# An SSM-convolution and SwiGLU gate, forward and backward in one program: the DFT matrices of the backward convolution turned on TensorE, its first loads in another order, one store on another queue

## The chip, the cores and the metric

The program runs on one core of a Trainium2 chip. The metric is the device time of one execution in microseconds (us), the median of the timed runs, lower is better. A profile is one execution taken by the hardware profiler; its span runs from the first to the last instruction.

## The reference

Only the part that the change touches is shown. `x` is 2048 tokens by 576 channels; `K` is a convolution kernel of 2048 taps for each channel, made from the SSM parameters.

```python
def _fwd_reference(...):
    xn = _layernorm(x, axis=-1)
    s = _A_ref(xn, ...)                 # y = causal convolution of xn with K (by FFT), plus xn * Dskip
    g = _silu(_B_ref(xn, w1, w3, w2))   # out = (silu(xn w1) * (xn w3)) w2, F = 4608
    return x + s * g

def reference(...):
    _out, _vjp = jax.vjp(_f, A_u, A_A_re, ..., B_w1, B_w3, B_w2)
    return (_out, *_vjp(grad_out))      # the output and the gradients of all twelve inputs
```

The backward pass needs `gs = grad_out * g`, the gradient that enters the convolution. From it come the gradient of `xn` and that of `K`, both by the same kind of convolution.

## The kernel before, in words

The convolution is done in blocks of 512 tokens (`LS`), four blocks (`NB`), each block of four tiles (`KT`) of 128 tokens. A block's spectrum is a product with cosine and sine matrices of 512 by 512, held in SBUF as tiles of 128 partitions by 4 by 512 in bf16. There are two kinds. `dC` and `dS` belong to the kernel's own transform (line 868) in the forward pass; the backward pass needs the same two matrices transposed, for the way back from the spectrum to taps (`idft_pair`, line 893). `cCS` belongs to the transform of the tokens; it is folded, 512 KB in all, is kept in DRAM as `CS_dram` from the prologue on, and is loaded again for the backward pass as `cCSb` (line 1301).

The program runs through these stages, with the times of the profiled execution:

- a prologue, then the first SwiGLU product (`ffn_hidden`, lines 1120 and 1128: `pgu`) woven with the making of the taps and, from about 400 to 530 us, with the forward convolution (`ssm_conv`, `conv_half`). For each half of the channels, `inverse(m)` for m = 3, 2, 1, 0 adds up products of spectra on VectorE (`V`) and goes back to tokens on TensorE (line 903). ScalarE copies one PSUM tile out (`ev`, line 1023), VectorE adds and subtracts the other (lines 1025 and 1026).
- the second SwiGLU product (`ffn_output`, about 545 to 697 us): for each of 16 token tiles i, 72 matmuls at line 1216 with a transposed load of H (`hcA`, `hcB`, `hcC`) as weights. `finish` follows on VectorE and stores `gs_t` (line 1237) and the output `o0` (line 1244).
- the backward pass (`backward`, from about 685 us): 18 groups of the SwiGLU gradients (`phase6_group` and what follows it), into which the backward convolution is woven by quarters g = 0 to 3 of the channels (`conv_bwd_quarter`), and then the parameter gradients and the input's gradient (line 1965) to the end.

The convolution's quarter 0 begins with the transform of `gs` (`dft_folded`, lines 879 to 884): twelve groups of four matmuls for blocks 0, 1 and 2, each group copied out by ScalarE (line 884); block 3 comes later, since its tokens (`gs_end`, kept in SBUF) are the last made. `fold` (lines 1375 to 1380) makes the difference `gm` and the sum `gs` of mirrored tiles on VectorE first. `a` and `az` are the two parts of the stored input spectrum (`UH_dram`); `spectrum_variants` (lines 909 to 911) prepares them on VectorE.

Every engine works its instructions in program order. The order of the work on each engine comes from priorities: `self.at(us)` sets a due time for what is recorded next, and `issue_after` holds an instruction behind another. A DMA is issued by an engine's queue, and an engine's queue (SP's, which carries most loads and stores, and POOL's) holds everything behind an issue that waits. DMAs of SP's queue share eight completion semaphores in turn, so each issue also waits for the landing of the DMA eight before it.

The transposed matrices `idC` and `idS` come about like this before the change: `dft_kernel_matrices` stores `dC` and `dS` to `D_dram`, and `dft_turn_kernel` loads them back with eight transposing DMAs, one behind each H load of tiles 5 and later.

`et_ps` is a PSUM tag with three buffers of one bank each. The forward convolution and the backward convolution both take their PSUM tiles from such a pool of three, and `pgu` has two buffers of two banks.

Of the kernel before, what the change touches and what calls it, by code (L numbers as in the profile page):

```python
# [13 lines left out]
FP32 = mybir.dt.float32  # L14
BF16 = mybir.dt.bfloat16
I32 = mybir.dt.int32
I16 = mybir.dt.int16
P = 128
# [82 lines left out]
class K:  # L101
# [722 lines left out]
    def dft_kernel_matrices(self, sb, half):  # L824
        nc, LS = self.nc, self.cfg.LS
        if half == 0:
            self.dC = self.matp.tile([P, 4, LS], BF16, name="dC")
            self.dS = self.matp.tile([P, 4, LS], BF16, name="dS")
        t = sb.tile([P, 2], FP32, name="dft_tk")
        fr = sb.tile([P, 2, LS], FP32, name="dft_frk")  # L830
        q = sb.tile([P, 2, LS], FP32, name="dft_qk")
        sl = slice(2 * half, 2 * half + 2)
        for i in range(2):
            with self.tc.issue_after(self.v_last.ins):
                nc.vector.tensor_scalar(out=t[:, i:i + 1], in0=self.ptok[:], scalar1=float((2 * half + i) * P), scalar2=None,
                                        op0=ALU.add)
            nc.scalar.activation(out=fr[:, i, :], in_=self.irow[:, 0:LS], func=ACT.Identity, scale=t[:, i:i + 1])
        self.wrap_turns(nc.vector, fr, q, 2.0 * LS)
        self.turn_sines(nc.scalar, self.dS[:, sl], self.dC[:, sl], fr, q)
        for i in range(2):  # L840
            nc.vector.tensor_copy(out=self.dS[:, 2 * half + i, 0:1], in_=self.sgnt[:])
        if half == 1:
            self.D_dram = self.dram.tile([2, 4, P, LS], BF16, name="D_dram")
            for m, mat in enumerate((self.dC, self.dS)):
                nc.sync.dma_start(out=self.D_dram[m].rearrange("i p k -> p i k"), in_=mat[:])

    def dft_turn_kernel(self):
        mats = []
        for m, tag in enumerate(("dC", "dS")):
            t = self.matp.tile([P, 4, self.cfg.LS], BF16, name="i" + tag, tag=tag)  # L850
            for i in range(4):
                with self.tc.issue_after(self.hc_loads[5 + 4 * m + i].ins):
                    self.nc.sync.dma_start_transpose(out=t[:, :, i * P:(i + 1) * P], in_=self.D_dram[m, i])
            mats.append(t)
        self.dC, self.dS = mats

    def dpieces(self):
        D = self.cfg.D
# [72 lines left out]
    def ssm_conv(self, T0, TC, ps, ps1):  # L931
        with self.pool(name="c_u", bufs=1) as up, \
                self.pool(name="c_k", bufs=1) as kp, \
                self.pool(name="c_raw", bufs=2) as rp, \
                self.pool(name="c_y", bufs=2) as ypool, \
                self.pool(name="c_tmp", bufs=2) as tp, \
                self.pool(name="c_s", bufs=3) as spool, self.pool(name="c_e", bufs=2) as epool:
            self.s_stores = []
            half = [self.conv_half(h, T0, kp, up, rp, ypool, tp, spool, epool, ps) for h in range(2)]
            NB = self.cfg.NB  # L940
            for b in range(NB):
                half[0]["dft"](b)
                half[0]["take"](b)
            for m in (3, 2):
                half[0]["inverse"](m)
            for m in (1, 0):
                half[1]["dft"](1 - m)
                half[0]["inverse"](m)
            for b in range(NB):
                if b > 1:  # L950
                    half[1]["dft"](b)
                half[1]["take"](b)
            for m in range(NB - 1, -1, -1):
                half[1]["inverse"](m)

    def conv_half(self, h, T0, kp, up, rp, ypool, tp, spool, epool, ps):
        nc, cfg = self.nc, self.cfg
# [187 lines left out]
    def ffn_output(self, T0, TB):  # L1145
        nc, cfg = self.nc, self.cfg
# [8 lines left out]
        with ExitStack() as es:  # L1155
# [64 lines left out]
            def finish(st):  # L1220
# [9 lines left out]
                with self.tc.issue_after(self.h_last.ins):  # L1230
# [3 lines left out]
                nc.vector.tensor_tensor(out=got, in0=gos[:], in1=e[:], op=ALU.mult)  # L1234
                gs_t = ip.tile([P, D], BF16, name="gs_t")
                nc.vector.tensor_tensor(out=p4(gs_t[:]), in0=n4(go_t[:]), in1=n4(g[:]), op=ALU.mult)
                nc.sync.dma_start(out=self.GS_dram[:, :, i, :].rearrange("g p d -> p g d"),
                                  in_=gs_t[:].rearrange("p (g d) -> p g d", g=4))
                if i >= LT - cfg.KT:
                    nc.scalar.copy(out=self.gs_end[:, i - LT + cfg.KT], in_=gs_t[:, 0:D // 4])  # L1240
                nc.vector.tensor_tensor(out=n4(g[:]), in0=p4(s_t[:]), in1=n4(g[:]), op=ALU.mult)
# [39 lines left out]
    def ssm_bwd_conv(self, T0, TQ, ps):  # L1281
        nc, cfg = self.nc, self.cfg
        D, LT = cfg.D, cfg.LT
        self.gK_dram = self.dram.tile([4, 2, P // 2, D // 64, 2, 2, 8 * LT], BF16, name="gK_dram")
        with self.pool(name="b_g", bufs=1, side="right") as self.bgp, \
                self.pool(name="b_k", bufs=1, side="right") as kp, self.pool(name="b_z", bufs=2, side="right") as zp:
            self.at(T0)
            self.lcol = kp.tile([P, LT], FP32, name="lcol")
            nc.vector.tensor_scalar(out=self.lcol[:], in0=self.irow[:, 0:LT], scalar1=float(P),
                                    scalar2=self.ptok[:, 0:1], op0=ALU.mult, op1=ALU.add)  # L1290
            nc.vector.tensor_scalar(out=self.lcol[:], in0=self.lcol[:], scalar1=1.0 / 512, scalar2=None, op0=ALU.mult)
            self.at(T0 - 100)
            self.dft_turn_kernel()
            W = D // 4
            for b in range(cfg.NB):
                kp.tile([P, 1, 2, cfg.KT, W], BF16, name=f"a2_{b}")
                kp.tile([P, 1, cfg.KT, W], BF16, name=f"az_{b}")
            kp.tile([P, cfg.NB, 2, W], BF16, name="gm")
            self.cCS = kp.tile([P, 2, 2, cfg.LS], BF16, name="cCSb")
            with self.tc.issue_after(self.hc_loads[5].ins):  # L1300
                nc.sync.dma_start(out=self.cCS[:], in_=self.CS_dram[:].rearrange("m i p k -> p m i k"))
            for g in range(4):
                yield from self.conv_bwd_quarter(g, kp, zp, ps, T0 + g * TQ, TQ)

# [38 lines left out]
    def conv_bwd_quarter(self, g, kp, zp, ps, T0, TQ):  # L1343
# [9 lines left out]
        for b in range(NB - 1 if g == 0 else 1):  # L1353
            ts = slice(b * KT, (b + 1) * KT) if g == 0 else slice(0, LT)
            if g == 0:
                self.at(T0 - 170 + 40 * b)
            nc.sync.dma_start(out=gs[:, ts], in_=self.GS_dram[g, :, ts])
        self.at(T0 if g else T0 - 100)
        for b in range(NB):
            A2[b] = kp.tile([P, 1, 2, KT, W], BF16, name=f"a2_{b}")  # L1360
            Az[b] = kp.tile([P, 1, KT, W], BF16, name=f"az_{b}")
            sync = Chain(self.tc, nc.sync)
            sync.prev = (ld if b else None) if g else self.hc_loads[2 * b + 4]
            sync.dma_start(out=A2[b][:, 0, 0], in_=self.UH_dram[g, b, :, 0])
            ld = sync.dma_start(out=Az[b][:, 0], in_=self.UH_dram[g, b, :, 1])
        G = [None] * NB
# [814 lines left out]
```

## Time and profile before

| | us |
|---|---|
| median of the timed runs (3) | 1768.03 |
| lowest and highest of them | 1760.42 and 1770.57 |
| the profiled execution's own time | 1755.63 |
| its span | 1753.7 |
| VectorE busy, share of the span | 1360.8, 78% |
| ScalarE busy | 890.6, 51% |
| TensorE busy 680 to 720 us | 29.5 of 40 |
| TensorE busy 720 to 760 us | 38.4 of 40 |

The profiled execution is shorter than all three timed runs. Busy times of TensorE count a matmul from its issue to its modelled end, so neighbours overlap; the distance between the starts of equal instructions is the better measure of a pace. Times within the program, such as "at 707 us", count from the span's start.

### The profile page before, as it was taken

The numbers are of one execution on the slowest core, as the hardware profiler recorded it, in microseconds if no ns is written. First come the engines' busy times: TensorE is split into PE (matmuls) and PEld (weight loads), VectorE is DVE, ScalarE is ACT, GpSimd is POOL, SyncE is SP. The second block draws the span as 40 slices with busy tenths as digits, with TensorE's granted clock in tenths as the row PEclk, the third lists the DMA queues.
The fourth block names the chain that finished last, engine by engine and source line by source line (L and its number), as shares of the span: only waits on it lengthen the run. The fifth ranks groups of instructions, "written<-read, shape, count | busy, mean of one in ns | idle before, by whom it ended". The sixth has DMA issues, their size and how long they took to land. (4 is left out here: it accounts for less than half of the span.)

```text
span 1753.7 us, 34702 instructions
## 1 busy us (share of the span) xinstructions
PE 1623.7 (93%) x13708; PEld 1196.8 (68%) x13765; DVE 1360.8 (78%) x2221; ACT 890.6 (51%) x1437; POOL 329.5 (19%) x530
## 2 busy tenths in 40 slices
PE   5889998999998999799999999999999998899997
PEld 2444444454545777678888888888888776678886
DVE  7658888879694555786976989759999975888675
ACT  4878889876862113665765657565444511001001
POOL 3101111112232110111011011111111133132132
PEclk9989999999999999999999999999999999999999
DMA  7779999978799998757676585679999999999991
GB/s 208 271 249 361 357 347 358 367 254 253 254 275 239 238 227 180 217 172 215 193 197 190 156 241 177 177 207 277 242 252 230 214 256 201 236 247 220 211 232 47
DMA packets 633769, 414.02 MB, mean 236 GB/s; under 512 B 427478, under 2 KB 578246, under 8 KB 628998
## 3 DMA queue, kind: packets, MB, share of 16 engines
q1 hardware_dynamic: 586780, 285.38, 65.8%
q0 software_dynamic: 32704, 114.32, 19.8%
q10 hardware_dynamic: 14122, 12.10, 2.5%
q8 instruction: 108, 1.77, 0.4%
q14 instruction: 55, 0.45, 0.1%
HBM read 130.88 MB, written 191.94 MB: 184 GB/s over the span
## 5 line engine op out<-in xcount | busy, mean ns | idle before, releaser
L1120 PE MATMUL pgu<-wmB_w,xnT 128*128 128x512 bf16 x1101 | 269.5, 379 | 5.6 <-ACT gu_t L1133 2.4
L1965 PEld LDWEIGHTS <-acts 128*128 128x128 bf16 x2304 | 226.0, 99 | 64.2 <-DMA acts<-GG_dram 3.3
L1913 PEld LDWEIGHTS <-xn_bf 128*128 128x128 bf16 x2304 | 224.9, 98 | 34.9 <-issue 8.6
L1496 DVE TENSOR_TENSOR pr_q<-et_ps,pz 128x1024 f32<-128x1024 f32 x144 | 176.0, 1222 | 35.3 <-PE et_ps L1491 24.4
L1965 PE MATMUL px<-wT,acts 128*128 128x288 bf16 x1472 | 192.9, 289 | 0.0
L1120 PEld LDWEIGHTS <-xnT 128*128 128x128 bf16 x1152 | 106.9, 98 | 120.4 <-issue 21.3
L1499 DVE TENSOR_REDUCE S_all<-pr_q 128x32 f32<-128x1024 f32 x144 | 175.3, 1217 | 3.1
L1852 PE MATMUL ph<-w2T,goT 128*128 128x256 bf16 x1440 | 171.1, 273 | 5.2 <-ACT gh L1855 5.2
L1852 PEld LDWEIGHTS <-goT 128*128 128x128 bf16 x1440 | 139.3, 98 | 23.3 <-issue 7.3
L1894 PE MATMUL pgw<-go_o,h_n 128*128 128x288 bf16 x1152 | 148.8, 286 | 0.0
L1133 ACT CAST gu_t<-pgu 128x1024 bf16<-128x1024 f32 x144 | 147.3, 1023 | 0.0
L1913 PE MATMUL pgw<-gu_n,xn_bf 128*128 128x256 bf16 x1152 | 133.7, 275 | 6.9 <-ACT gw L1896 6.3
L1894 PEld LDWEIGHTS <-h_n 128*128 128x128 bf16 x1152 | 112.0, 98 | 29.4 <-issue 2.0
L1913 PE MATMUL pgw<-gg_n,xn_bf 128*128 128x256 bf16 x1152 | 130.5, 273 | 0.0
L1132 ACT ACTIVATE s_t<-pgu 128x512 bf16<-128x512 f32 x144 | 87.8, 610 | 83.7 <-PE pgu L1120 44.4
L1141 POOL DMA_DIRECT2D GUF_dram<-gu_t x72 | 65.5, 910 | 339.7 <-ACT gu_t L1133 312.4
L1965 PE MATMUL px<-wA,acts 128*128 128x288 bf16 x832 | 110.3, 289 | 5.2 <-DMA acts<-GG_dram 2.7
L1916 ACT CAST gw<-pgw 128x512 bf16<-128x512 f32 x72 | 42.6, 591 | 140.8 <-PE pgw L1913 139.8
L1855 ACT CAST gh<-ph 128x512 bf16<-128x512 f32 x144 | 83.0, 608 | 58.7 <-PE ph L1852 50.9
L2032 ACT ACTIVATE go<-gx 128x576 bf16<-128x576 f32 x15 | 10.2, 683 | 190.8 <-DVE gx L2013 190.8
L1136 DVE TENSOR_TENSOR h_t<-s_t,gu_t 128x1024 bf16<-128x1024 bf16 x72 | 49.5, 688 | 47.8 <-ACT gu_t L1133 46.8
L1897 POOL DMA_DIRECT2D out_dram<-gw x36 | 20.2, 562 | 345.5 <-ACT gw L1896 269.7
(329 smaller groups left out, 3019.4 us busy)
## 6 DMA issues: line engine op xcount, KB each, us to landing
GUF_dram<-gu_t POOLq DMA_DIRECT2D x72, 512.0 KB, 5.6
H_dram<-h_t SPq DMA_DIRECT2D x72, 256.0 KB, 5.5
Q_dram<-q_k SPq DMA_DIRECT2D x36, 512.0 KB, 3.9
gg_n<-GUF_dram POOLq DMA_DIRECT2D x18, 1024.0 KB, 6.0
h_n<-GUF_dram POOLq DMA_DIRECT2D x18, 1024.0 KB, 8.6
GG_dram<-gg_n SPq DMA_DIRECT2D x36, 512.0 KB, 10.3
GU_dram<-gu_n SPq DMA_DIRECT2D x36, 512.0 KB, 5.3
E_dram<-E_k SPq DMA_DIRECT2D x54, 256.0 KB, 2.3
```

The lines of the kernel that those rows point to most:

```text
L1120: ins = nc.tensor.matmul(pt, lhsT=xnT[:, c, ts], rhs=wm[w][:, c, :], start=(q == 0 and c == 0), stop=(q == 1 and c == nfull - 1))
L1132: nc.scalar.activation(out=s_t[:, :, q, :], in_=pg.rearrange("p (g f) -> p g f", g=ng), func=ACT.Silu)
L1133: nc.scalar.copy(out=gu_t[:, :, :, q, :], in_=pgu[:].rearrange("p k (g f) -> p k g f", g=ng))
L1136: self.h_last = nc.vector.tensor_tensor(out=h_t[:].rearrange("p t (g f) -> p g t f", g=ng), in0=s_t[:], in1=gu_t[:, 1], op=ALU.mult)
L1141: self.u_stores[step] = nc.gpsimd.dma_start(out=self.GUF_dram[fb * ng:(fb + 1) * ng, :, :, i0:i0 + NT, :].rearrange("g p k t f -> p k g (t ...
L1496: nc.vector.tensor_tensor(out=pr[:].rearrange("p r k e -> p r (k e)"), in0=T[x][:].rearrange("p k z d a -> p (k z d a)")[:, None].to_broad ...
L1499: nc.vector.tensor_reduce(out=self.S_all[:, :, d0:d0 + 4], in_=pr[:].rearrange("p r k (d a) -> p (r k) d a", d=4), op=ALU.add, axis=AX.X)
L1852: self.pe_last = nc.tensor.matmul(ph[j][:, k, :].rearrange("p (a f) -> p a f", f=P), lhsT=lw, rhs=rh, start=(n == 0), stop=(n == nfull))
L1855: self.sc(lambda: nc.scalar.copy(out=gh[:, j], in_=ph[j][:]))
L1894: self.pe_last = nc.tensor.matmul(pgw[pi_][:, 0:pw], lhsT=hn[:, tt, fl * P:(fl + 1) * P], rhs=go_o[:, tt, po:po + pw], start=(tt == 0), st ...
L1913: self.pe_last = nc.tensor.matmul(pw_[:, c % 2], lhsT=self.xn_bf[:, tt, c * P:(c + 1) * P], rhs=nat[:, tt, :], start=(tt == 0), stop=(tt = ...
L1965: self.pe_last = nc.tensor.matmul(px[pi_][:, 0:pw], lhsT=acts[i][:, ai, fi, :], rhs=w[:, po:po + pw], start=(n == 0), stop=(n == len(steps ...
```

## The change

Three edits that go together:

1. `D_dram`, its two stores and the eight transposing loads are gone. `dft_turn_kernel` now transposes each matrix in place: 16 transposes of 128 by 128 on TensorE (data as weights, identity as the moving operand) into two `et_ps` tiles, seen as bf16, and two copies of 128x1024 by ScalarE back into the matrix. It is called twice in the forward convolution's second half: after `inverse(3)` for `dC`, and after `inverse(2)` for `dS`, each with a due time 8 us behind that inverse's.
2. The backward convolution's first loads: `cCSb`, which was issued behind the eight loads of `a` and `az`, comes ahead of them, right behind the three loads of `gs`.
3. The store of `gs_t` for the last tile (i = 15) goes to GpSimd's queue; the other fifteen stay on SP's.

```diff
-        if half == 1:
-            self.D_dram = self.dram.tile([2, 4, P, LS], BF16, name="D_dram")
-            for m, mat in enumerate((self.dC, self.dS)):
-                nc.sync.dma_start(out=self.D_dram[m].rearrange("i p k -> p i k"), in_=mat[:])
-
-    def dft_turn_kernel(self):
-        mats = []
-        for m, tag in enumerate(("dC", "dS")):
-            t = self.matp.tile([P, 4, self.cfg.LS], BF16, name="i" + tag, tag=tag)
-            for i in range(4):
-                with self.tc.issue_after(self.hc_loads[5 + 4 * m + i].ins):
-                    self.nc.sync.dma_start_transpose(out=t[:, :, i * P:(i + 1) * P], in_=self.D_dram[m, i])
-            mats.append(t)
-        self.dC, self.dS = mats
+
+    def dft_turn_kernel(self, ps, mat):
+        nc, KT = self.nc, self.cfg.KT
+        halves = []
+        for j in range(0, KT, 2):
+            pt = ps.tile([P, 512], FP32, name="et_ps")[:].bitcast(BF16).rearrange("p (j i q) -> p j i q", j=2, q=P)
+            for k in range(2):
+                for i in range(KT):
+                    nc.tensor.transpose(pt[:, k, i], mat[:, i, (j + k) * P:(j + k + 1) * P], self.ident_bf[:])
+            halves.append((j, pt))
+        for j, pt in halves:
+            nc.scalar.copy(out=mat[:, j:j + 2].rearrange("p j (i q) -> p j i q", q=P), in_=pt)
...
             for m in range(NB - 1, -1, -1):
                 half[1]["inverse"](m)
+                if m > 1:
+                    self.at(T0 + self.CONV_INVERSES[1][m] + 8)
+                    self.dft_turn_kernel(ps, (self.dC, self.dS)[NB - 1 - m])
...
-                nc.sync.dma_start(out=self.GS_dram[:, :, i, :].rearrange("g p d -> p g d"),
-                                  in_=gs_t[:].rearrange("p (g d) -> p g d", g=4))
+                (nc.sync if i < LT - 1 else nc.gpsimd).dma_start(out=self.GS_dram[:, :, i, :].rearrange("g p d -> p g d"),
+                                                                 in_=gs_t[:].rearrange("p (g d) -> p g d", g=4))
...
-            self.at(T0 - 100)
-            self.dft_turn_kernel()
...
-            with self.tc.issue_after(self.hc_loads[5].ins):
-                nc.sync.dma_start(out=self.cCS[:], in_=self.CS_dram[:].rearrange("m i p k -> p m i k"))
...
-            nc.sync.dma_start(out=gs[:, ts], in_=self.GS_dram[g, :, ts])
+            ld = nc.sync.dma_start(out=gs[:, ts], in_=self.GS_dram[g, :, ts])
         self.at(T0 if g else T0 - 100)
+        if g == 0:
+            with self.tc.issue_after(ld.ins):
+                ld = nc.sync.dma_start(out=self.cCS[:], in_=self.CS_dram[:].rearrange("m i p k -> p m i k"))
...
-            sync.prev = (ld if b else None) if g else self.hc_loads[2 * b + 4]
+            sync.prev = ld if b or g == 0 else None
```

On SP's queue, at the passage from `ffn_output` to the backward pass, the order before was this (`GS_dram` is the store of the last tile's `gs_t`):

```order
L1237 DMA GS_dram<-gs_t 128x4x144
L1357 DMA gs<-GS_dram 128x576 x2
L86 DMA a_0_8564<-UH_dram 128x576
L86 DMA az_8565<-UH_dram 128x576
L86 DMA a_1_8568<-UH_dram 128x576
L86 DMA az_8569<-UH_dram 128x576
L86 DMA a_2_8572<-UH_dram 128x576
L86 DMA az_8573<-UH_dram 128x576
L86 DMA a_3_8576<-UH_dram 128x576
L86 DMA az_8577<-UH_dram 128x576
L1301 DMA cCSb<-CS_dram 128x4x512
L1357 DMA gs<-GS_dram 128x576
```

And it is now, at the same place of SP's queue (`out_dram` is the store of the last tile but one's output `o0`, `odd_out` that of the last tile's):

```order
L1245 DMA out_dram<-o_8328 128x576
L1354 DMA gs<-GS_dram 128x576 x3
L1358 DMA cCSb<-CS_dram 128x4x512
L86 DMA a_0_8591<-UH_dram 128x576
L86 DMA az_8592<-UH_dram 128x576
L86 DMA a_1_8595<-UH_dram 128x576
L86 DMA az_8596<-UH_dram 128x576
L86 DMA a_2_8599<-UH_dram 128x576
L86 DMA az_8600<-UH_dram 128x576
L86 DMA a_3_8603<-UH_dram 128x576
L86 DMA az_8604<-UH_dram 128x576
L1245 DMA odd_out_109<-o_8435 128x576
```

The store of the last `gs_t` no longer stands ahead of the loads, the third load of `gs` has moved up to the other two, and `cCSb` has moved ahead of the eight `a` and `az`. In the built program the first `gs` load waits for the last tile's last product with `w2a` (line 1216, the 32nd of its 72 matmuls), the first `a` for a product some 20 matmuls later, and the last `az` for VectorE's sum `o0` of the last tile (line 1243); this is so before and after.

On ScalarE, at the forward convolution's `inverse(1)` of the second half, the order before was this (`s_t` and `gu_t` empty the two banks of `pgu`, `ev` empties the even part of an inverse):

```order
L1132 ACTIVATE s_t<-pgu 128x2x256
L1133 CAST gu_t<-pgu 128x4x256
L1023 COPY ev<-et_ps 128x288 x2
L1132 ACTIVATE s_t<-pgu 128x2x256
L1133 CAST gu_t<-pgu 128x4x256
```

And it is now, with the transposed `dS` copied out ahead of both `ev`:

```order
L1133 ACTIVATE s_t<-pgu 128x2x256
L1134 CAST gu_t<-pgu 128x4x256
L853 COPY dS<-et_ps 128x1024 x2
L1024 COPY ev<-et_ps 128x288 x2
L1133 ACTIVATE s_t<-pgu 128x2x256
L1134 CAST gu_t<-pgu 128x4x256
```

On TensorE the 16 transposes of `dS` stand between the end of a `pgu` and the four matmuls of `inverse(1)`'s even part; those of `dC` stand between two `pgu` products, two SwiGLU steps behind `inverse(3)`, with no inverse near. On POOL's queue the store of the last `gs_t` stands behind the load of `h_n` for group 0 and ahead of the load of `h_n` for group 1.

## The prediction

> **What bounds the kernel now.** I read the page's head first, then the waits of TensorE, then the order of time on each engine at the longest wait that the change could touch.
>
> ```profile
> span 1753.7 us, 34702 instructions
> PE 1623.7 (93%) x13708; PEld 1196.8 (68%) x13765; DVE 1360.8 (78%) x2221; ACT 890.6 (51%) x1437; POOL 329.5 (19%) x530
> PE et_ps L1491 <- DVE pr_q L1496: 11.7, 20, 2.2
> ...
> PE et_ps L882 <- DMA cCSb<-CS_dram: 7.3, 1, 7.3
> ```
>
> TensorE is busy 93% of the span, so time is gained where TensorE stands still or has less to do. The lower rows are from the waits (who waited, for whom, total us, times, longest). The last is one single wait of 7.3 us, for the load of `cCSb`, the matrix that the change moves forward. TensorE's own order of time shows the place:
>
> ```profile
> 691.43 1.63 PE L1216 MATMUL po<-w2g,hcA 128*128 128x288 bf16 x12
> ...
> 705.48 1.80 PE L1852 MATMUL ph<-w2T,goT 128*128 128x256 bf16 x15 [1.40 <-ACT gh L1855]
> 714.61 0.42 PE L882 MATMUL et_ps<-gs,cCSb 128*128 128x144 bf16 x2 [7.33 <-DMA cCSb<-CS_dram]
> ```
>
> TensorE is idle from 707.28 to 714.61. The queue of SP shows why the load came late:
>
> ```profile
> 690.74 0.34 SPq L1244 DMA_DIRECT2D out_dram<-o  x1
> 701.30 0.37 SPq L1237 DMA_DIRECT2D GS_dram<-gs_t  x1
> 701.77 1.65 SPq L1357 DMA_DIRECT2D gs<-GS_dram  x2
> 703.50 0.38 SPq L86 DMA_DIRECT2D a<-UH_dram  x1
> ...
> 709.33 0.32 SPq L86 DMA_DIRECT2D az<-UH_dram  x1
> 710.09 0.38 SPq L1301 DMA_DIRECT2D cCSb<-CS_dram  x1
> ```
>
> SP issues nothing from 691 to 701.30: the store of the last `gs_t` heads the queue and waits for VectorE. Then ten loads go ahead of `cCSb`, and with eight semaphores in turn it also waits for the first `a`, eight places ahead (6.6 us from 703.50 to 710.09). `cCSb` itself needs 4.5 us. During SP's stillness the DMA engines are free: in forty slices of 0.875 us from 690 on, slices 4 to 13 (692.6 to 701.4) move nothing.
>
> ```profile
> GB/s 173 61 108 0 0 0 0 0 0 0 0 0 0 23 160 37 180 377 393 387 351 384 373 329 133 151 360 324 57 0 0 140 187 365 412 178 221 353 16 128
> ```
>
> **The gap, step by step.** With the store on POOL's queue, SP goes on after the output store of 690.74. The first `gs` load waits for the last tile's matmuls with `w2a`, which stand before the row of 691.43, so it goes at about 691.6; three loads at about 0.8 us (1.65 for two) put `cCSb` at 694. After 4.5 us it lands near 698.5, and at 702 even with the 6.6 us of a slow one. TensorE needs it at 707.28. So that wait goes, and the next late thing is VectorE's folding, which must give sum and difference of block 0:
>
> ```profile
> 706.32 0.30 DVE L1379 TENSOR_TENSOR gm<-gs 128x288 bf16<-128x288 bf16 x1
> 706.54 0.69 DVE L1827 TENSOR_TENSOR h_n<-gu_n,h_n 128x1024 bf16<-128x1024 bf16 x1
> 709.27 0.31 DVE L1379 TENSOR_TENSOR gm<-gs 128x288 bf16<-128x288 bf16 x1 [2.04 <-DMA gs<-GS_dram]
> 709.50 0.52 DVE L1380 TENSOR_TENSOR gs<-gs 128x288 bf16<-128x288 bf16 x2
> ```
>
> In the new order two more `gm` follow L1827 (done 707.23), then the first sum: at 0.23 each, the sum stands at about 707.9, and TensorE starts at 708.0 instead of 714.61. What follows is set by ScalarE, which empties twelve PSUM tiles:
>
> ```profile
> 715.31 1.36 ACT L884 CAST g<-et_ps 128x288 bf16<-128x288 f32 x3 [9.39 <-PE et_ps L882]
> 716.92 0.88 ACT L884 CAST g<-et_ps 128x288 bf16<-128x288 f32 x2 [0.25 <-PE et_ps L882]
> 718.04 0.40 ACT L884 CAST g<-et_ps 128x288 bf16<-128x288 f32 x1 [0.25 <-PE et_ps L882]
> 718.76 1.91 ACT L884 CAST g<-et_ps 128x288 bf16<-128x288 f32 x6 [0.32 <-PE et_ps L882]
> 720.56 1.06 ACT L1823 ACTIVATE gg_n<-gg_n 128x1024 bf16<-128x1024 bf16 x1
> ```
>
> The casts are 4.55 us of work with 0.8 us of gaps, during which the granted clock was low (0.50 until 717, 0.64 until 720, in the windows below):
>
> ```profile
> 700.00:707.00 7.00, 5.60 (x52) 4.88 (x50) 7.00 (x15) 5.53 (x8) 2.57 (x5) 1.00 0.55 171
> 714.60:717.00 2.40, 2.39 (x20) 2.31 (x21) 0.62 (x2) 1.28 (x4) 0.56 (x1) 0.50 0.04 13
> 717.00:720.00 3.00, 2.99 (x29) 2.71 (x28) 0.00 (x0) 2.35 (x8) 0.00 (x0) 0.64 0.86 238
> ```
>
> (Columns: stretch, length, busy time of PE, PEld, DVE, ACT, POOL, then the granted clock.) In 700 to 707 TensorE paused twice, by about 1.5 us, and the clock stayed at 1.00; so the remaining pause of 0.7 us should leave it whole. I take 0.3 us of gaps, and 0.45 us from the first matmul to the first cast (0.70 before, at the half clock): 708.0 + 0.45 + 4.55 + 0.3 = 713.3, against 720.67 before. **The gap gives 7.4 us.** VectorE's next step, L1826, waits for the activation of 720.56, so it comes earlier by the same amount, and TensorE's next matmuls (L1894, L1852) wait for nothing else. Bounds: 7.7 if TensorE starts at once at 707.3 (and VectorE folds faster than I think); 5.9 if SP is still held until 701.3, since three `gs` and then `cCSb` would be out at 704.2 and land at 708.7, 709.2 at most, instead of 714.6.
>
> What is queued behind the moved issues: the eight `a` and `az` stand behind `cCSb`, but now go from 694 on. The last `az` still waits for VectorE's last `o0`, 703.95, and lands in about 6 us, at 710; the copies that wait for it must be done at 714, ahead of L1826. On POOL, the load of `h_n` for group 1 now stands behind the store, both about 702.5 before; one more issue there costs about 0.6 us, and that tile's readers come after 735. The next quarter's `gs` load (720.13 before) now waits for the store on POOL, issued near 701.4. None of this reaches TensorE, and I put it at 0; uncovered, it would cost what lands after 714.
>
> **The transposes in the forward convolution.** The trace has transposes of the same form, from the prologue:
>
> ```profile
> 56.27 0.61 PE L250 MATMUL t_ps<-ident_bf,xn_bf 128*128 128x128 bf16 x8
> 56.71 0.59 PE L615 MATMUL e_ps<-sel_val,lhs_r 128*128 128x512 bf16 x2
> L1277 PE MATMUL ptr<-ident_bf,go_o x75: 219/219/243, 559.7 to 693.2; 128*128 128x128 bf16 x60, 128*64 128x128 bf16 x15
> ```
>
> Eight take 0.44 us until the next matmul, 0.055 each: 16 take 0.9 us, 32 take 1.8. Between 480 and 530 TensorE has no gap to put them in (below), so they count in full. ScalarE's copies of 128x1024 bf16 from PSUM are not in the trace; the nearest rows are these (the second number of each pair is the mean of one in ns):
>
> ```profile
> L1133 ACT CAST gu_t<-pgu 128x1024 bf16<-128x1024 f32 x144 | 147.3, 1023 | 0.0
> L1278 ACT COPY goT<-ptr 128x512 bf16<-128x512 bf16 x15 | 8.8, 587 | 72.8 <-PE ptr L1277 72.8
> ```
>
> By the first one takes 1.0 us, by twice the second 1.2. I take 1.0. For `dC` both are hidden: ScalarE uses 1.6 us of each 2.05 us `pgu`, two copies set it back by about 0.5 us behind two PSUM buffers of `pgu`. `dS` is different:
>
> ```profile
> 517.53 1.90 PE L1120 MATMUL pgu<-wmB_w,xnT 128*128 128x512 bf16 x8
> 519.27 1.63 PE L903 MATMUL et_ps<-V,cT 128*128 128x288 bf16 x12
> 521.33 0.65 PE L903 MATMUL et_ps<-V,cT 128*128 128x288 bf16 x4 [0.42 <-ACT ev L1023]
> 522.03 1.67 PE L1120 MATMUL pgu<-wmB_w,xnT 128*128 128x512 bf16 x7
> 519.47 0.60 ACT L1132 ACTIVATE s_t<-pgu 128x512 bf16<-128x512 f32 x1 [0.54 <-PE pgu L1120]
> 519.97 1.01 ACT L1133 CAST gu_t<-pgu 128x1024 bf16<-128x1024 f32 x1
> ```
>
> Now (from 519.27 as zero): transposes 0 to 0.9, filling two of three PSUM tiles; even part 0.9 to 1.45 in the third; ScalarE is busy with `pgu` until 1.6, copies at 1.6 and 2.55. The odd part needs the first tile, free at 2.6; the next even part the second, free at 3.55; the last odd part follows, and the next `pgu` starts at 4.75 instead of 2.76. So `dS` costs 2.0, with `dC` 0.9: **2.9 us in all**. VectorE, which feeds this stage, is no bound: the row of 519.27 names no wait for it. Bounds: above, the pace of the transposes at L1277 (five in 0.49 us, 0.098 each: 3.1) with 1.1 of stall at `dS` and 0.5 at `dC`, 4.8 us; below, 1.8 with no stall.
>
> Below that only if the delay is swallowed later. The next wait on the way is at 570:
>
> ```profile
> 570.35 6.74 PE L1216 MATMUL po<-w2a,hcA 128*128 128x288 bf16 x32 [4.25 <-DMA hcA<-H_dram]
> ```
>
> That load was issued at 549.58, when TensorE had freed its buffer, and what fills the DMA queues ahead of it is also issued on TensorE's progress; so I let it move with TensorE and swallow 0 (bound: all 2.9).
>
> **What is taken away.** The two stores to `D_dram` (290 us) and eight transposing loads of 1.2 us of SP's time each lie beside TensorE that does not wait for them:
>
> ```profile
> 580.20 1.91 SPq L853 DMA_TRANSPOSE idC<-D_dram  x1
> 600.00:650.00 50.00, 50.00 (x415) 39.60 (x413) 29.07 (x43) 7.61 (x16) 8.09 (x15) 1.00 1.10 227
> ```
>
> From 600 to 650 TensorE is busy 50.00 of 50.00 us while five of the loads run. Gain 0; around 290 it is ScalarE, not a DMA, that TensorE waits for.
>
> **Sum.** -7.4 + 2.9 = -4.5 us. The profiled execution took 1755.63, so 1751.1 for such a one. It is 12.4 us below the median of the three timed runs, 1768.03, which are what the result is compared with: **1763.5**. From about 735 us on everything hangs on what came before, so I carry the shift to the end. The bounds together give -5.9 (7.7 and 1.8) to -1.1 (5.9 and 4.8).
>
> **The rivals.**
>
> *The delay is swallowed at 570.* If the DMA queues ahead of `hcA` are emptied meanwhile, the wait of 4.25 shrinks by 2.9 and only the 7.4 remains: 1760.6. If the shorter pause also keeps the clock up there, the 32 matmuls (6.74 us there, 4.3 at the pace of the twelve of 691.43) win 2.4 more: 1758.2. For it: that load takes 20.8 us to land. Against: its forerunners move along.
>
> *The transposes do not overlap*, the case that ends slower. If each starts only when the last one is out of the array, the price is 0.219 us, the duration at L1277: 32 make 7.0, with 1.1 of stall 8.1, and the sum is +0.7: 1768.7. It decides above 0.195 us each (7.4 less 1.1, over 32). The rows at 56.27 speak against it: 0.055, at a clock of 1.00. A page of the Trainium skill, TensorE: Matmul & The Clock Gate, Part 4 (PE-mode transpose), speaks against this change: a transpose took about 275 ns inside a kernel, and the full clock is not granted for such work. By its price 32 would be an estimated 8.8 us and the change 2.5 us slower. The trace does not bear it out, for the eight of 56.27 keep a pace of 55 ns.
>
> *The gain is lost on the way.* From 1300 to 1500 us VectorE and loads share the chain, and an earlier TensorE could meet them: between 0 and -4.5, about 1767.
>
> **Chances.** Forecast 0.62; swallowed 0.18; lost on the way 0.14; transposes in a row 0.06. About 0.5%, 8.8 us, is what a measurement of this kernel can tell from no change. The timed runs lie 10 us apart, so I add some 4 us either way: the swallowed case reaches faster by 0.5% in about half of its share, the forecast in a sixth: 0.21. Slower by 0.5% needs +8.8, beyond every case but through the spread: 0.06. The rest, 0.73, is within. The range goes from 1753 (swallowed, with the spread) to 1771 (nothing left, with the spread).
>
> **What would show it.** Right: `cCSb` issued near 694; no wait for it at line 880; L880 begins near 708 with a clock of 1.00; L1823 near 713 plus the 3 us from before; in the convolution some 0.9 us for `dC` and 2.0 for `dS`, with waits for the copies at line 853. Wrong: SP idle until 701; a wait for `gs`, `gm` or `az`; transposes at over 0.1 us each; another wait at 570.

## The result, and the profile after

| | before | changed |
|---|---|---|
| median of 22 timed runs | 1764.32 | 1756.01 |
| lowest and highest | 1755.19 and 1784.39 | 1739.01 and 1774.62 |
| profiled execution, span | 1753.7 | 1762.1 |

The ratio is 0.9938, with a 95% interval from 0.9917 to 0.9959: 10.9 us less, between 7.2 and 14.6. It leaves out, as slow, every run more than 1.5% above the fastest of its kernel (six of the changed kernel's 22 and one of before's, and six of before's 35 beside four of the experiments), so that ratios and medians differ; with every run kept the medians lie 8.3 us apart. The changed kernel was timed twice more beside the experiments, on two chips: ratios of 0.9967 [0.9934, 0.9999] and 0.9908 [0.9875, 0.9942]. With all 46 runs kept, and each set against the mean of the before runs on its own chip, the mean difference is 8.3 us, with a standard error of about 1.5. So it is faster, by some 8 us, where 4.5 had been forecast.

The profiled execution of the changed kernel is an unlucky one, 8.4 us longer than that of before. Its head and four of its waits of TensorE (who waited, for whom, total us, times, longest):

```profile
span 1762.1 us, 34759 instructions
PE 1621.4 (92%) x13740; PEld 1195.7 (68%) x13797; DVE 1361.0 (77%) x2221; ACT 893.4 (51%) x1441; POOL 329.5 (19%) x531
PE po L1217 <- DMA hcC<-H_dram: 9.5, 1, 9.5
...
PE et_ps L901 <- ACT dS L853: 1.4, 2, 1.1
...
PE et_ps L880 <- DMA az<-UH_dram: 0.7, 1, 0.7
```

The wait of 7.3 us for `cCSb` is gone, 0.7 is left in its place, the copies of `dS` cost 1.4, and a new wait of 9.5 us for `hcC` has come. Line numbers have moved by one or two: 1216 is 1217 now, 882 is 880, 903 is 901.

**The gap.** On TensorE, SP, VectorE and ScalarE, by the order of time:

```profile
697.79 1.63 PE L1217 MATMUL po<-w2g,hcA 128*128 128x288 bf16 x12
...
714.29 0.28 PE L880 MATMUL et_ps<-gs,cCSb 128*128 128x144 bf16 x2 [0.66 <-DMA az<-UH_dram]
```

```profile
697.98 1.27 SPq L1354 DMA_DIRECT2D gs<-GS_dram  x3
699.29 0.43 SPq L1358 DMA_DIRECT2D cCSb<-CS_dram  x1
```

```profile
713.94 0.74 DVE L1380 TENSOR_TENSOR gs<-gs 128x288 bf16<-128x288 bf16 x3
714.74 1.00 ACT L882 CAST g<-et_ps 128x288 bf16<-128x288 f32 x3 [2.47 <-PE et_ps L880]
...
715.94 2.82 ACT L882 CAST g<-et_ps 128x288 bf16<-128x288 f32 x9 [0.20 <-PE et_ps L880]
718.65 1.06 ACT L1823 ACTIVATE gg_n<-gg_n 128x1024 bf16<-128x1024 bf16 x1
```

Tile 15 comes 6.4 us later here, so distances count, from the twelve matmuls with `w2g` on (691.43 before, 697.79 now). `cCSb` goes out 1.5 us behind them; TensorE starts 16.5 behind (23.2 before), once VectorE's first sum of the row of 713.94 is made (the profile names the load of `az`; SP issued the last `az` at 710.33, and the first matmuls read `gs` and `cCSb`; in d_last, one of the experiments below, it names VectorE's sum `gs` for the same wait, 0.67 us). ScalarE's activation stands at 20.86, where before it stood at 720.56 - 691.43 = 29.13: **8.3 us gained**. The clock stays whole:

```profile
714.30:717.00 2.70, 2.58 (x33) 2.19 (x33) 2.28 (x14) 2.06 (x7) 0.43 (x1) 1.00 0.13 42
717.00:720.00 3.00, 3.00 (x34) 2.50 (x32) 0.28 (x2) 3.00 (x8) 0.13 (x1) 1.00 0.70 175
```

The granted clock (third number from the end) is 1.00 in both stretches, where it had been 0.50 and 0.64.

**The transposes.** TensorE in the forward convolution's second half, and ScalarE's four copies:

```profile
502.70 1.06 PE L850 MATMUL et_ps<-ident_bf,dC 128*128 128x128 bf16 x16
503.60 1.89 PE L1121 MATMUL pgu<-wmB_w,xnT 128*128 128x512 bf16 x8
...
518.43 1.06 PE L850 MATMUL et_ps<-ident_bf,dS 128*128 128x128 bf16 x16
519.33 0.65 PE L901 MATMUL et_ps<-V,cT 128*128 128x288 bf16 x4
521.10 0.65 PE L901 MATMUL et_ps<-V,cT 128*128 128x288 bf16 x4 [1.12 <-ACT dS L853]
522.02 1.14 PE L901 MATMUL et_ps<-V,cT 128*128 128x288 bf16 x8 [0.27 <-ACT dS L853]
523.21 1.67 PE L1121 MATMUL pgu<-wmB_w,xnT 128*128 128x512 bf16 x7
```

```profile
504.29 1.95 ACT L853 COPY dC<-et_ps 128x1024 bf16<-128x1024 bf16 x2
520.02 1.95 ACT L853 COPY dS<-et_ps 128x1024 bf16<-128x1024 bf16 x2
```

Sixteen transposes take 0.90 us until the next matmul, 0.056 each. From the transposes of `dS` to the next `pgu` it is 4.78 us. All inverses of this half, from the first matmul to the last one's end, take 37.8 us, 34.9 before: **2.9 us lost**.

**The H loads.** The two terms make -5.4. The rest of this execution's +8.4 stands elsewhere: the stages ahead are 1.7 us shorter, and from the last inverse's end to the twelve `w2g` matmuls, which I call the **H stretch**, it takes 168.0 us, 162.8 before; from the activation to the end 1043.5, 1033.1 before. TensorE and SP around the longest wait:

```profile
679.20 6.79 PE L1217 MATMUL po<-w2a,hcC 128*128 128x288 bf16 x32 [9.49 <-DMA hcC<-H_dram]
```

```profile
646.26 10.02 SPq L1775 DMA_TRANSPOSE hcB<-H_dram  x1
656.38 0.53 SPq L1238 DMA_DIRECT2D GS_dram<-gs_t  x1
657.00 2.54 SPq L1775 DMA_TRANSPOSE w2T<-w2r  x2
659.63 0.53 SPq L1245 DMA_DIRECT2D out_dram<-o  x1
660.26 3.49 SPq L1775 DMA_TRANSPOSE w2T<-w2r  x2
663.84 1.95 SPq L1754 DMA_DIRECT2D w2r<-in_B_w_dram  x4
665.84 8.54 SPq L1775 DMA_TRANSPOSE hcC<-H_dram  x1
```

SP is occupied without a break, single H loads hold it for 8 to 10 us, and with the loads of `w2T` in between, that of `hcC` comes too late; the 32 matmuls behind the wait take 6.79 us at a granted clock of 0.59 (679.2 to 686 us), against 4.08 for the 32 of the next tile at 693.87, at 1.00. Is this the change, or chance? That, and what the loads of `idC` and `idS` that are gone had cost beside the H loads, is what the experiments ask.

### The profile page after: what moved, and what is told of

It is laid out like the page before. It is cut to its first block, busy times and chain, and to the rows that moved or that the text cites. A ratio compares the mean times of both kernels' runs of the same rounds, so it can differ in the third digit from the quotient of the medians.

```text
span 1762.1 us, 34759 instructions
## 1 busy us (share of the span) xinstructions
PE 1621.4 (92%) x13740; PEld 1195.7 (68%) x13797; DVE 1361.0 (77%) x2221; ACT 893.4 (51%) x1441; POOL 329.5 (19%) x531
## 5 line engine op out<-in xcount | busy, mean ns | idle before, releaser
L1499 DVE TENSOR_REDUCE S_all<-pr_q 128x32 f32<-128x1024 f32 x144 | 175.3, 1217 | 3.1
```

The source lines that it names most:

```text
L1499: nc.vector.tensor_reduce(out=self.S_all[:, :, d0:d0 + 4], in_=pr[:].rearrange("p r k (d a) -> p (r k) d a", d=4), op=ALU.add, axis=AX.X)
```

## The experiments

All runs in one table. The first number is the difference of the medians, in us, to the kernel before on the same chip, with all runs kept; then the ratio with its interval, and from each kernel's one profile: the inverses, the H stretch, the way from the `w2g` matmuls to the activation, and from there to the end. again, loads_only, no_turn and d_three ran on one chip, d_act, d_late, d_twice and ds_later on a second, again_2, no_turn_2, d_last and turn_early on a third.

| kernel | us | ratio | inverses | H stretch | to activation | to the end |
|---|---|---|---|---|---|---|
| before | | | 34.9 | 162.8 | 29.1 | 1033.1 |
| changed | -8.3 | 0.9938 [0.9917, 0.9959] | 37.8 | 168.0 | 20.9 | 1043.5 |
| again | -4.7 | 0.9967 [0.9934, 0.9999] | 37.8 | 154.0 | 20.9 | 1037.1 |
| again_2 | -12.3 | 0.9908 [0.9875, 0.9942] | 37.8 | 156.8 | 20.9 | 1041.7 |
| loads_only | -9.1 | 0.9945 [0.9912, 0.9978] | 34.9 | 170.7 | 20.9 | 1038.5 |
| no_turn | -16.6 | 0.9903 [0.9868, 0.9937] | 34.9 | 158.0 | 20.9 | 1026.4 |
| no_turn_2 | -14.5 | 0.9890 [0.9839, 0.9941] | 34.9 | 159.5 | 20.9 | 1038.7 |
| d_twice | +5.3 | 1.0033 [1.0003, 1.0063] | 34.9 | 166.6 | 28.8 | 1026.9 |
| d_three | +39.5 | 1.0230 [1.0177, 1.0282] | 34.9 | 201.8 | 28.9 | 1039.9 |
| d_act | -6.0 | 0.9979 [0.9944, 1.0015] | 34.9 | 176.9 | 20.9 | 1023.4 |
| d_late | -10.5 | 0.9964 [0.9933, 0.9994] | 34.9 | 159.8 | 28.4 | 1025.7 |
| d_last | -6.9 | 0.9967 [0.9926, 1.0007] | 34.9 | 158.5 | 20.9 | 1045.3 |
| ds_later | -1.0 | 1.0013 [0.9974, 1.0053] | 39.2 | 162.2 | 20.9 | 1032.4 |
| turn_early | -5.9 | 0.9947 [0.9916, 0.9977] | 37.8 | 159.3 | 20.9 | 1036.1 |

**loads_only: the gap alone.** Parts 2 and 3 of the change put on the kernel before; part 1 left out.

> The kernel before with parts 2 and 3 of the change alone (cCSb ahead of the a and az loads, the last gs_t store on GpSimd); the matrices still go through D_dram. Theory A (the local terms are all there is: the gap gives 7.4 to 8.5 us, the transposes cost 3, the DMAs that fell away gave nothing): 7 to 9 us faster than the kernel before, and faster than the changed kernel by about 3; no wait for cCSb, the first activation at the old line 1823 comes about 21 us after the last product with w2a, not 29. Theory B (the eight transposing loads that fell away held up the loads of H, and their going is worth another 3 to 6 us): the same 7 to 9 us here, but level with the changed kernel or slower by up to 3, since the transposing loads are still there.

The gap's gain stands by itself: 20.9 us to the activation, and 9.1 us faster. Its H stretch, with the eight loads at their old place, is 170.7 us long, with waits of TensorE for `hcC` and `hcA`:

```profile
PE po L1216 <- DMA hcC<-H_dram: 9.3, 2, 8.6
...
PE po L1216 <- DMA hcA<-H_dram: 2.8, 1, 2.8
```

**no_turn and no_turn_2: what the transposes cost, and the loads that they replaced.** This is the changed kernel without the transposes and their copies; the backward pass then works with untransposed matrices, so this step of the computation is left out.

```diff
-                if m > 1:
-                    self.at(T0 + self.CONV_INVERSES[1][m] + 8)
-                    self.dft_turn_kernel(ps, (self.dC, self.dS)[NB - 1 - m])
```

> The changed kernel without the 32 transposes and the four copies: the two matrices stay untransposed, which leaves this part of the computation out. There are neither transposing loads nor transposes. Theory A: 3 us faster than the changed kernel (0.9 for dC, 2.0 for dS), so 7 to 9 faster than before, level with loads_only. Theory B: also 3 faster than the changed kernel, but 3 to 6 us faster than loads_only, 11 to 14 faster than before.

> The changed kernel without transposes and copies once more (the matrices stay untransposed). Theory D: 8 to 12 us faster than before. Theory E: 15 to 18 faster, as at first. Profile by either: 34.9 us for the inverses, an H stretch of 154 to 168 us.

Both are 14 to 17 us faster than before. Against loads_only, on the same chip, no_turn is 7.4 us faster by the medians, though all that it lacks is the two stores to `D_dram` and the eight transposing loads: more than theory B's 3 to 6, and not A's level. no_turn_2, 14.5 faster than before, lies between theory D's 8 to 12 and E's 15 to 18.

**again and again_2: the changed kernel twice more.**

> The changed kernel once more, on the same chip as the other three and with a second profile. Theory A: 4.5 to 5.5 us faster than before. Theory B: 7 to 11 faster. In the profile either expects 0.9 us at dC, 2.0 at dS and no wait for cCSb; the wait for hcC at 679 us (9.5 us in the first profile of the changed kernel) should be absent or stand elsewhere if it is chance, and at the same load again if the change made it.

> The changed kernel a third time, beside no_turn_2 on the same chip. In the first pair the two lay some 12 us apart, though the profiles show only 2.9 us of it, in the forward convolution. Theory D (the transposes cost the 2.9 us that stand there, the rest of the 12 was scatter of the H loads and of the parameter gradients behind 1200 us): 4 to 9 us faster than before and 1 to 6 us slower than no_turn_2. Theory E (the transposes have a further price that stands elsewhere): 4 to 9 faster than before, 8 to 15 slower than no_turn_2. Profile by either: 37.8 us for the inverses of the second half, 20.7 us from the last product with w2a to the activation.

The wait of 9.5 us for `hcC` was chance: again has no wait for H at all, again_2 one of 2.7 at another tile. Three profiles of this one kernel have H stretches of 168.0, 154.0 and 156.8. The times are as far apart: again, 4.7 us faster than before, met theory A's 4.5 to 5.5, and again_2, 12.3 faster, went beyond the 4 to 9 expected. Two cases look like this on SP, again first, then again_2:

```profile
605.08 4.41 SPq L1775 DMA_TRANSPOSE hcA<-H_dram  x1
...
614.41 4.43 SPq L1775 DMA_TRANSPOSE hcB<-H_dram  x1
```

```profile
612.81 10.54 SPq L1775 DMA_TRANSPOSE hcA<-H_dram  x1
...
625.59 7.99 SPq L1775 DMA_TRANSPOSE hcB<-H_dram  x1
```

In the first case an H load holds SP for 4.4 us of each 9.3 us tile, and SP waits for the next buffer. In the second the same instruction holds it for 8 to 10.5 us, the two stores between the loads end 0.4 us ahead of the second load, and there is no slack left. The same kernel shows both, and other executions lie between: 4.5 to 6.2 us in that of before, from 583 to 648 us. The transposes' further cost stays open: again was 11.8 us slower than no_turn by the medians (theory E), again_2 only 2.2 slower than no_turn_2 (theory D), and each profile shows 2.9.

**d_three and d_twice: more transposing loads.** In d_three each of the eight is issued three times; in d_twice each tile has one of `idC` and one of `idS`, to slices that no neighbouring tile writes (sixteen in all).

```diff
-                    self.nc.sync.dma_start_transpose(out=t[:, :, i * P:(i + 1) * P], in_=self.D_dram[m, i])
+                    for _ in range(3):
+                        self.nc.sync.dma_start_transpose(out=t[:, :, i * P:(i + 1) * P], in_=self.D_dram[m, i])
```

> The kernel before with each of the eight transposing loads of idC and idS issued three times: sixteen more of the kind that the change removes. Theory A (they lie beside TensorE that does not wait): no change, within 2 us, and waits for H loads between 545 and 690 us of the same size as before, one of about 4 us. Theory B (they hold up the H loads): 6 to 12 us slower, with more or longer waits of TensorE for hcA, hcB or hcC.

> The kernel before with two transposing loads per tile in place of one (the second of the other matrix, to a slice that is written by another tile's load, so that no load waits for the one just ahead of it, as they did in d_three, where the second and third wrote the same slice). Theory B1 or B2: 3 to 10 us slower than before, H stretch 168 to 180 us. Theory A or C: no change within 3 us; the 39 us of d_three then came from the loads waiting for one another, not from their number.

d_three lost 39.5 us, all of it in the H stretch. But part of that is the experiment's own doing, as its SP queue shows:

```profile
611.55 1.35 SPq L854 DMA_TRANSPOSE idC<-D_dram  x1
...
615.70 4.66 SPq L854 DMA_TRANSPOSE idC<-D_dram  x2
620.46 4.80 SPq L1776 DMA_TRANSPOSE hcC<-H_dram  x1
```

The second load is issued 4.2 us behind the first, whose slice it writes again, and the H load stands behind them. d_twice, where the two write different slices, is free of that: its second load goes out 1.2 to 2.0 us behind the first. Eight loads more cost 5.3 us by the medians, within theory B's 3 to 10; the interval of the ratio reaches from 0.5 to 11 us, so that it excludes no change, though not the upper end of theory A's 3. Its H stretch of 166.6 us lies just below the 168 to 180 expected.

**d_act: the same loads on ScalarE's queue.** The diff is against loads_only.

```diff
-                with self.tc.issue_after(self.hc_loads[5 + 4 * m + i].ins):
-                    self.nc.sync.dma_start_transpose(out=t[:, :, i * P:(i + 1) * P], in_=self.D_dram[m, i])
+                with self.tc.issue_after(self.sgos[2 + 4 * m + i].ins):
+                    self.nc.scalar.dma_start_transpose(out=t[:, :, i * P:(i + 1) * P], in_=self.D_dram[m, i])
```

> loads_only with the eight transposing loads of idC and idS on ScalarE's queue, one behind each sgo activation of tiles 2 to 9, so at about the same times; SP's queue has none of them. Theory B1 (it is the issue on SP's queue that they cost: about 1.9 us of the 9.3 us that each tile has there, so that a late H load catches up more slowly): the stretch from the forward convolution's end to the last product with w2a takes 154 to 160 us, as without these loads, and the kernel is 3 to 8 us faster than loads_only, 12 to 17 faster than before. Theory B2 (the transposing loads take the DMA engines from the H loads): 163 to 171 us there, as in loads_only, and 7 to 10 us faster than before. Theory C (the waits for H come and go by chance, whatever stands in the queue): no difference from loads_only beyond 4 us, and an H stretch anywhere from 154 to 171 us.

It does not tell B1 from B2, for it made a wait of its own: its H stretch of 176.9 us lies beyond all three forecasts. ScalarE's queue and the work behind it:

```profile
584.97 1.31 ACTq L853 DMA_TRANSPOSE idC<-D_dram  x1
586.32 0.59 ACT L1278 COPY goT<-ptr 128x512 bf16<-128x512 bf16 x1 [17.54 <-DMA GS_dram<-gs_t]
586.96 0.65 ACT L1224 ACTIVATE sgo<-po 128x576 f32<-128x576 f32 x1
...
591.92 0.85 PE L1277 MATMUL ptr<-ident_bf,go_o 128*128 128x128 bf16 x5 [5.06 <-DVE go_o L1234]
```

In the built program each of these loads waits for H loads of SP's queue to land, and ScalarE, which must empty `po` (`sgo`), stands still for 17.5 us until it is out (the profile names an earlier store); in turn, SP's next H load goes out 2.5 to 3.8 us behind each of the eight; TensorE then waits for `go_o`, which VectorE makes from `sgo`. The Trainium skill, DMA: Bandwidth & Descriptors, section Silent corruption: two transposing streams in flight at once, asks that a second stream of transposing DMAs wait for the first one's completion; the waits agree with that rule, and what happens without them was not tried.

**d_late and d_last: the loads moved out of the H stretch, in place of transposes.** Both are loads_only with the eight behind another load of SP: the last H load in d_late (its diff against loads_only is below), the last `az` of quarter 0 in d_last.

```diff
-                with self.tc.issue_after(self.hc_loads[5 + 4 * m + i].ins):
+                with self.tc.issue_after(self.hc_loads[-1].ins):
```

> loads_only with all eight transposing loads behind the last H load (tile 15), on SP's queue: they take some 10 to 15 us of it from about 675 us on, when SP has little else to do, and no transposes on TensorE are needed. Theories B1 and B2: H stretch 154 to 160 us, as without these loads; no 2.9 us for transposes; 12 to 17 us faster than before, 3 faster than the changed kernel on average. Against it: the stores of gs_t for tiles 13 to 15 stand behind the eight loads; if VectorE then waits for a gs_t buffer, or cCSb comes late again, up to 8 us are lost and it is 5 to 9 faster than before. Theory C: as loads_only, 7 to 10 us faster than before.

> loads_only with the eight transposing loads behind the last az load of quarter 0, at some 711 us, when SP has nothing to do: no transposes on TensorE, no transposing loads of D_dram beside the H loads, and the gs_t stores stay free, which d_late held up (4.7 us of TensorE's time). The taps' way back needs idC from some 745 us on; on TensorE it moves behind the next products. Theory B1: H stretch 154 to 162 us, 34.9 us for the inverses, 20.7 us to the activation; as fast as no_turn_2, 10 to 17 us faster than before, and so faster than the changed kernel by 3 to 10. Against it: the loads of w2T for the next group stand behind the eight and come some 10 us later; if TensorE then waits, up to 5 us are lost. Theory C (the loads beside H cost nothing): as loads_only, 7 to 10 faster than before.

Both H stretches are short (159.8 and 158.5), and each kernel paid elsewhere. In d_late it is what the expectation named against it; SP, VectorE and TensorE:

```profile
679.28 6.87 SPq L853 DMA_TRANSPOSE idC<-D_dram  x4
686.20 6.46 SPq L853 DMA_TRANSPOSE idS<-D_dram  x4
692.76 0.53 SPq L1237 DMA_DIRECT2D GS_dram<-gs_t  x1
```

```profile
695.08 0.76 DVE L1236 TENSOR_TENSOR gs_t<-go_t,g 128x576 bf16<-128x576 bf16 x1 [7.61 <-DMA GS_dram<-gs_t]
```

```profile
697.90 0.85 PE L1277 MATMUL ptr<-ident_bf,go_o 128*128 128x128 bf16 x5 [4.73 <-DVE go_o L1234]
```

The store of `gs_t` stood behind eight loads of 1.7 us, VectorE waited for its buffer, and 7.5 us of the gap's gain were lost again (28.4 to the activation). That it is still 10.5 us faster speaks for the H stretch's part, though its one profile shows only 3.0 us of it there. In d_last the gap is whole, but the load of `gg_n` for the next group, issued at 711.36 while the eight and `w2T` were under way, let ScalarE start on it only at 724.91:

```profile
724.91 1.28 ACT L1820 ACT_TABLE_LOAD   x1 [10.50 <-DMA gg_n<-GUF_dram]
```

```profile
730.43 9.63 PE L1914 MATMUL pgw<-gu_n,xn_bf 128*128 128x256 bf16 x64 [9.44 <-ACT gw L1897]
```

TensorE waits 9.44 us there, and d_last, 6.9 us faster than before, missed the 10 to 17 expected. No version that computes the whole result was shown to beat the changed kernel.

**ds_later and turn_early: another place for `dS`.** In ds_later `dS` is transposed ahead of `inverse(2)` by due time, but recorded behind it; in turn_early, whose diff against the change is below, both matrices are due behind `inverse(3)`.

```diff
-                if m > 1:
-                    self.at(T0 + self.CONV_INVERSES[1][m] + 8)
-                    self.dft_turn_kernel(ps, (self.dC, self.dS)[NB - 1 - m])
+                if m > 2:
+                    for n, mat in enumerate((self.dC, self.dS)):
+                        self.at(T0 + self.CONV_INVERSES[1][m] + 8 + 7 * n)
+                        self.dft_turn_kernel(ps, mat)
```

> The changed kernel with dS transposed some 20 us earlier in due time, ahead of inverse(2) and between two pgu products as dC is, not right ahead of inverse(1). By the prediction's working the stall of 1.1 us at dS goes: the second half's inverses take 36.7 us from first to last in place of 37.8 (34.9 without transposes). If the copies on ScalarE were not the cause of that stall, 37.8 stays. The median says little of 1 us: 6 to 12 us faster than before in either case.

> The changed kernel with both matrices transposed behind inverse(3), dS between two pgu products like dC, and taking its PSUM tiles ahead of inverse(2)'s, which ds_later did not (there it took them behind, and TensorE waited 2.1 us for them in the middle of a pgu). By the prediction's working dS then costs 0.9 as dC does: 36.7 us for the inverses of the second half, against 37.8 in the changed kernel and 39.2 in ds_later. Time: 5 to 10 us faster than before; 1 us isn't seen in it.

Neither saved the 1.1 us. In ds_later half of `dS` had to wait for a PSUM tile that VectorE still read, in the middle of a `pgu`; in turn_early `dS` ended up right ahead of `inverse(2)`, with the same stall as in the change. The first row is of ds_later, the second of turn_early:

```profile
517.85 0.61 PE L850 MATMUL et_ps<-ident_bf,dS 128*128 128x128 bf16 x8 [2.07 <-DVE s_t L1027]
```

```profile
514.01 0.65 PE L901 MATMUL et_ps<-V,cT 128*128 128x288 bf16 x4 [1.12 <-ACT dS L853]
```

So the stall goes with the neighbourhood of an inverse, not with this one place; a place with a `pgu` on both sides, as `dC` has, was not hit. ds_later, 1.0 us faster than before where 6 to 12 had been expected, was a clear miss: its inverses take 1.4 us longer than the change's, and the rest is not explained.

## Why the prediction was right, and where it was too small

The forecast time was 1763.5 us, and 1756.0 was measured. Of these 7.5 us, 3.7 lie in the reference: the median of before was 1768.03 from three runs and is 1764.32 from 22. The other 3.8 are the gain, 8.3 in place of 4.5.

*The gap: right.* Forecast 7.4 us, measured 8.3, and 20.9 us to the activation in ten profiles out of ten whose loads and stores were arranged as in the change or freer (d_late, which held up the stores of `gs_t`, aside). TensorE's start was forecast 16.6 us behind the `w2g` matmuls and came 16.5 behind. The difference lies in ScalarE's casts: 0.2 us of gaps in place of 0.3, and 3.8 us in place of 4.55 in the rows. A single cast takes 0.40 us before and 0.41 now, so the 4.55 taken for work held short waits for the slow TensorE. The prediction's upper bound of 7.7 was passed; by its own terms a start at 707.3 gives 8.1. The wait that was to follow, VectorE's folding, followed, though the profile gives it the name of one of the signs of being wrong, `az`.

*The transposes: right in their own stage.* 2.9 us forecast, 2.9 measured there in all three profiles of the change (37.8 less 34.9), 0.9 for `dC` and 2.0 for `dS`, with a longest wait of 1.1 us for the copies. The pace of 0.056 us each at a clock of 1.00 settles the rival of 0.219. The price of about 275 ns that the Trainium skill gives (TensorE: Matmul & The Clock Gate, Part 4, PE-mode transpose) isn't met here either.

*What was taken away: a term put at nothing, probably too low.* The prediction put the eight transposing loads at "Gain 0", because TensorE is busy 50.00 of 50.00 us while they run. That row is of an execution in which SP had kept up. The loads sit in the queue of the H loads, and that queue has little to spare: when H loads hold SP for 8 to 10 us each, a delay isn't made up, and TensorE waits tiles later. In nine profiles without these loads in the H stretch it lasts 159.6 us on average (154.0 to 168.0), in the two with eight on SP 162.8 and 170.7, in d_twice 166.6. The means differ by 7 us, with few profiles and a standard deviation of 4 us among the nine. More than half of it is one wait, always for the `hcC` that stands behind the loads of `w2T`: 8.6 us in loads_only, 7.1 in d_twice, 9.5 in the first profile of the change, and none above 0.6 in before or the other eight. The medians don't agree on it: no_turn is 7.4 us faster than loads_only and d_twice 5.3 slower than before, which speaks for a large term; again is 4.4 slower than loads_only, which speaks for none. The change as a whole, 8.3 us faster, is what the gap alone gave; if the transposes took 2.9 of it, some 3 us are left for this term, and none if they were swallowed. That the loads cost something is supported by d_twice and no_turn; the size, anywhere up to 7 us, is not settled, nor whether it is the issue on SP's queue or the DMA engines that the loads take from H.

*The rival at 570* (the delay is swallowed at the first whole H load) is borne out in part. The prediction let the load of `hcA`, and what stands ahead of it, move along with TensorE, and named another wait at 570 as a sign of being wrong. The 4.25 us there are gone in all three profiles of the change, while seven of the nine kernels without transposes wait 2.1 to 4.2 us. From the first matmul of the inverses to that product it is 73.35 us in all three, and 73.6 on average (70.4 to 76.7) in the nine: with 2.9 us put in, TensorE comes there no later. Two rows of SP, before and then changed:

```profile
531.89 2.55 SPq L1191 DMA_DIRECT2D w2g<-in_B_w_dram  x4
549.58 16.66 SPq L1775 DMA_TRANSPOSE hcA<-H_dram  x1
```

```profile
530.02 5.28 SPq L1192 DMA_DIRECT2D w2g<-in_B_w_dram  x4
550.76 7.22 SPq L1775 DMA_TRANSPOSE hcA<-H_dram  x1
```

TensorE's first product with `w2a` starts at 530.81 before and at 531.99 in the change. So the loads of `w2g` go out 1.1 us behind it before (0.4 to 1.1 in the nine) and 2.0 ahead of it in the change (in all three): the forerunners of `hcA` did not move along with TensorE. It is no proof that this took up the delay: no_turn, not delayed, has no wait there either, and ds_later and turn_early, whose `w2g` go out 0.3 to 0.4 us ahead, wait 3.8 and 1.0. *Lost on the way*, between 1300 and 1500 us, didn't happen as a rule: from the activation to the end the profiles scatter from 1023.4 to 1043.5 us with no order by kernel (d_last, with 1045.3, has its own wait of 9.44 there).

*What stays open.* What the transposes cost in the end. By the rival it is nothing, by their own stage 2.9 us, by the first pair (again and no_turn) 11.8 and by the second 2.2. Over all runs, each against the mean of before on its chip, no_turn is 6.9 us ahead of the changed kernel, with a standard error of some 2.5. The more the transposes cost, the more the loads that are gone must have given back; the gap's 8.3 us does not hang on it.

## What to carry to other kernels

A wait in one stage, with the resources in rows around it, can be forecast to a microsecond; whether a queue that feeds the neighbouring stage has slack cannot be read from one execution that ran well. Nor does a load move along with the engine that waits for it, unless what stands ahead of it in the queue does. Before a load is called hidden, add up what its in-order queue does per tile, and see how long the slowest of the loads there takes. And a load that is moved out of a full queue must be followed to the next instruction behind its new place: here a store of `gs_t` in one case, a load of `gg_n` in the other.

## What the runs showed of the hardware that had not been expected

The same transposing H load held SP's queue for 4.4 us in one execution of a kernel and for 10.5 in another. The scatter of the timed runs, 29 us between the fastest and the slowest of before, has its counterpart in the stages: 14 us in the H stretch of one unchanged kernel (154.0 to 168.0), and 20 us from the activation to the end over all kernels but d_last, while the inverses (34.9 or 37.8 us) and the way to the activation in the new arrangement (20.9) repeat to 0.1 us.
